# Sixteen matmuls that nobody reads, in TensorE's gaps at the end of a bandwidth-bound decode kernel

## The chip, the cores and the metric

The kernel runs on one core of a Trainium2 chip. The metric is the device time in microseconds (us) of one execution; a median over the runs of a set is quoted. Each run has a state: slow, for a program on one core, when it is over 1.5% above the fastest run of the same kernel, else fast; a single run has none. Ratios are the mean time of one kernel's fast runs over that of the other's of the same rounds, so not quite the ratio of the medians that stand beside them.

## The reference, cut to what matters

One decode step, cut to its outline: grouped-query attention over a long cache (part A), a small gated MLP (part B), and a gate that mixes the two.

```python
q = x @ wq                                    # 1 x 1024 -> 32 heads of 128
scores = einsum(q, k) * 128 ** -0.5           # 4 kv heads, 65536 cached tokens, 128 wide
a = softmax(scores) @ v ... @ wo              # wo: 4096 x 1024
b = mlp(x)                                    # w_in, w_out
return g * a + (1 - g) * b
```

What matters is the traffic: one token of query meets all of k_cache, v_cache, wq, w_in, w_out and wo, each read once. The profile counts 162.01 MB from HBM.

## The kernel before

All large operands go through one SBUF tile `kv` of five slots, loaded by one queue (SyncE) in program order. Each kv head has four K tiles and four V tiles. The end of the kernel is the part that the change touches:

```python
WO_SPLIT = ((16,), (8, 4, 2, 1, 1))
...
    for j, n, at in ((0, 2, 1), (2, 1, 3), (3, 1, 4)):       # the last head's V tiles
        for i, vt in enumerate(load_kv(A_v_cache, G - 1, j, at, n)):
            v_tile(G - 1, j + i, vt)
    head_out(G - 1)                                          # DVE chain and two small matmuls
    ...
    for at, split in enumerate(WO_SPLIT):
        for n in split:                                      # wo in pieces of 16, 8, 4, 2, 1, 1 rows
            t = load(wo_view[:, c0:c0 + n, :], (n, D), ...)
            project(t, n, oa, c0, last=(c0 + n == OC))       # 4 matmuls a row, 32 columns x 256
            c0 += n
    ...
    nc.scalar.copy(out=out_sb[:], in_=out_ps[:])             # eviction, then two small writes
```

The split of wo into ever smaller pieces means that only one row, four matmuls, stands after the last landing.

Of the kernel before, what the change touches and what calls it, by code (L numbers as in the profile page):

```python
# [8 lines left out]
FP32 = mybir.dt.float32  # L9
# [6 lines left out]
P = 128  # L16
# [6 lines left out]
ZN = 448  # L23
HN = 512
WO_SPLIT = ((16,), (8, 4, 2, 1, 1))


@with_exitstack
def kernel(
# [15 lines left out]
    nc = tc.nc  # L45

    _, _, D = A_x.shape
    _, G, S, DH = A_k_cache.shape
# [15 lines left out]
    assert S % (P * CT) == 0 and F == 2 * NB * ZN and ZN == B * FC and HD == NHB * NB * HN  # L64
    assert NHB * NB == 2 * G and CC * B == 2 * HN and sum(map(sum, WO_SPLIT)) == OC

# [5 lines left out]
    pss = ctx.enter_context(tc.tile_pool(name="pss", bufs=2, space=bass.MemoryType.PSUM))  # L72
# [6 lines left out]
    def same_weights(ins):  # L79
        held.add(ins.ins.name)  # L80
# [79 lines left out]
    def load(src, shape, at):  # L160
        n = 1
        for s in shape:
            n *= s
        v = kv[:, int(at * CT * P):int(at * CT * P) + n]
        if len(shape) == 2:
            v = v.rearrange("p (a b) -> p a b", b=shape[1])
        ins = nc.sync.dma_start(out=v, in_=src)  # L167
        if not first_load:
            first_load.append(ins.ins.name)
        return v  # L170

    def load_kv(src, g, j, at, n=1):
        h, i = divmod(j, 2)
        rows = src[0, g, 2 * h * CT * P:2 * (h + 1) * CT * P, :].rearrange(
            "(p c) d -> p (c d)", c=2 * CT)
        v = load(rows[:, i * CT * DH:(i + n) * CT * DH], (n * CT * DH,), at)
        return [v[:, i * CT * DH:(i + 1) * CT * DH] for i in range(n)]
# [26 lines left out]
    wt = [big.tile([P, VC, BP, NB, VC, REP], BF16, name=f"wt{i}") for i in range(2)]  # L204
# [15 lines left out]
    def one_hot(shape, dtype, in0, col, name):  # L220
# [13 lines left out]
                     start=True, stop=True)  # L234
# [107 lines left out]
    for k in range(NHB):  # L342
# [15 lines left out]
                     rhs=q4[:].rearrange("p t x -> p (t x)"), start=True, stop=True)  # L358
# [71 lines left out]
    def v_tile(g, j, vt):  # L430
        if j == 0:
            o_ps[g] = pso.tile([P, 2, VC * DH], FP32, name="o_ps")
        vx = vt.rearrange("p (v c d) -> p c v d", v=VC, d=DH)
        for u in range(CC // 2):
            hs = slice(u % 2 * P // 2, (u % 2 + 1) * P // 2)
            for e in range(2):
                ins = nc.tensor.matmul(  # L437
                    o_ps[g][hs, e, :],
                    lhsT=ptt[g, j][:, 2 * u:2 * u + 2, :].rearrange("p c x -> p (c x)"),
                    rhs=vx[:, 2 * u + e], start=(j == 0 and u < 2),  # L440
                    stop=(j == NT - 1 and u >= CC // 2 - 2), skip_group_check=True)
                if e > 0:
                    same_weights(ins)

    def head_out(g):
        gs = slice(g * B, (g + 1) * B)
        nc.vector.tensor_tensor(  # L447
            out=om8, in0=o_ps[g][:].rearrange("p e (v d) -> p (e v) d", d=DH),
            in1=own_8[:].unsqueeze(2).to_broadcast([P, 2 * VC, DH]), op=ALU.mult)
        o_sb = wk.tile([P, DH], FP32, name="o_sb")  # L450
        nc.vector.tensor_reduce(out=o_sb[:], in_=om8.rearrange("p x d -> p d x"), axis=AX.X,  # L451
                                op=ALU.add)
        om_ps = psm.tile([P, DH + NT], FP32, name="om_ps", tag="m")
        hs = hsel[:].rearrange("p h q -> p (h q)")
        nc.tensor.matmul(om_ps[gs, DH:], lhsT=hs, rhs=lss[g][:], start=True, stop=True,
                         skip_group_check=True)
        nc.tensor.matmul(om_ps[gs, :DH], lhsT=hs, rhs=o_sb[:], start=True, stop=True,  # L457
                         skip_group_check=True)
        rl = wk.tile([P, 2], FP32, name="rl")
        nc.vector.reduce_sum(out=rl[gs, 0:1], in_=om_ps[gs, DH:], axis=AX.X)  # L460
        nc.vector.reciprocal(out=rl[gs, 1:2], in_=rl[gs, 0:1])
        om = wk.tile([P, QD, OC], FP32, name="om")
        nc.vector.tensor_tensor(
            out=om[gs], in0=om_ps[gs, :DH].rearrange("p (q c) -> p q c", c=OC),
            in1=own_q[gs, :].unsqueeze(2).to_broadcast([B, QD, OC]), op=ALU.mult)
        osum = wk.tile([P, OC], FP32, name="osum")
        nc.vector.tensor_reduce(out=osum[gs, :], in_=om[gs].rearrange("p q c -> p c q"),
                                axis=AX.X, op=ALU.add)
        nc.vector.tensor_scalar(out=oa[gs, :], in0=osum[gs, :], scalar1=rl[gs, 1:2],
                                scalar2=gate[gs, :], op0=ALU.mult, op1=ALU.mult)  # L470

    NO = D // NB
    out_ps = psl.tile([P, NO], FP32, name="out_ps")

    def project(w, n, vec, c0, first=False, last=False):
        for c in range(n):
            for t in range(NB):
                nc.tensor.matmul(  # L478
                    out_ps[t * B:(t + 1) * B, :],
                    lhsT=vec[:, c0 + c:c0 + c + 1].to_broadcast([P, B]),  # L480
                    rhs=w[:, c, t * NO:(t + 1) * NO],
                    start=(first and c == 0), stop=(last and c == n - 1),
                    skip_group_check=True)
# [22 lines left out]
    for j, n, at in ((0, 2, 1), (2, 1, 3), (3, 1, 4)):  # L506
        for i, vt in enumerate(load_kv(A_v_cache, G - 1, j, at, n)):
            v_tile(G - 1, j + i, vt)
    head_out(G - 1)


    wo_view = A_wo.rearrange("(p c) n -> p c n", c=OC)
    c0 = 0
    for at, split in enumerate(WO_SPLIT):
        for n in split:
            t = load(wo_view[:, c0:c0 + n, :], (n, D), at + c0 % (OC // 2) * D / (CT * P))
            project(t, n, oa, c0, last=(c0 + n == OC))
            c0 += n
    out_sb = const.tile([P, NO], BF16, name="out_sb")
    out_rows = out.rearrange("o t (q n) -> (o t q) n", n=NO)  # L520
    nc.scalar.copy(out=out_sb[:], in_=out_ps[:])  # L521
    for i, queue in enumerate((nc.scalar, nc.sync)):
        p0 = (2 * i + 1) * B - 1
        ins = queue.dma_start(out=out_rows[2 * i:2 * i + 2, :], in_=out_sb[p0:p0 + 2, :])
# [40 lines left out]
```

## Time and profile before

| | before |
|---|---|
| median of the first three runs | 383.22 us (383.17 to 383.25) |
| HBM read | 162.01 MB at 425 GB/s over the span of 381.4 us |
| TensorE busy | 232.4 us, 61% |
| DVE busy | 218.4 us, 57% |
| last wo transfer lands | 378.88 us after the span's start |

Three more lines of the page; the first is what moved, the others the chain of work that ended last, as shares of the span by engine, and the eviction (its idle time before it, and what ended that):

```profile
HBM read 162.01 MB, written 0.00 MB: 425 GB/s over the span
...
DMA 59%; PE 20%; DVE 16%; issue 2%; ACT 1%; SPq 1%; DVEq 0%; ACTq 0%
...
L521 ACT CAST out_sb<-out_ps 128x256 bf16<-128x256 f32 x1 | 0.4, 372 | 45.4 <-PE out_ps L478 45.4
```

The chain lists PE at 20% and DVE at 16% because buffers in mid-kernel come free through them.

### The profile page before, as it was taken

To read this page: it belongs to the slowest core of one execution; us is meant where nothing else is said; L and a number is where in the kernel's file an instruction comes from. 1 tells how busy PE (TensorE), PEld (TensorE's weight loads), DVE (VectorE), ACT (ScalarE), POOL (GpSimd) and SP (SyncE) were. 2 spreads that over 40 slices of the span, in tenths; PEclk is the share of its full clock that TensorE was granted. 3 is DMA by queue.
4 is the path that set the end of the run, shared out by engine and by line. 5 is a ranking of instruction groups with operands and counts; after the bars stand their busy time and mean duration, and the time that the engine had idled before them with its cause. 6 is when DMAs were issued, how large, how long until landed. Compare 5 with 4: busy or idle time off the path is not lost.

```text
span 381.4 us, 2581 instructions
## 1 busy us (share of the span) xinstructions
PE 232.4 (61%) x1372; PEld 56.8 (15%) x796; DVE 218.4 (57%) x211; ACT 39.6 (10%) x55; POOL 4.4 (1%) x10
## 2 busy tenths in 40 slices
PE   0433467678157944796397629872967196849355
PEld 0110011112011210121011101120111011212123
DVE  4241487996687506966977059669780488550040
ACT  1010001111601100114010001050001010500000
POOL 4000000000000000000000000000000000000000
PEclk9966659998759895989588959895799679969766
DMA  9999999999999999999999999999999999999995
GB/s 376 439 426 416 433 436 440 436 461 429 400 426 440 440 435 426 440 440 440 440 428 440 440 440 433 428 427 406 433 440 428 426 433 427 440 411 436 440 405 230
DMA packets 4375, 162.17 MB, mean 425 GB/s; under 512 B 520, under 2 KB 524, under 8 KB 908
## 3 DMA queue, kind: packets, MB, share of 16 engines
q1 hardware_dynamic: 4324, 162.01, 98.7%
q8 instruction: 8, 0.13, 0.1%
q14 instruction: 3, 0.02, 0.0%
q10 hardware_dynamic: 40, 0.01, 0.0%
HBM read 162.01 MB, written 0.00 MB: 425 GB/s over the span
## 4 chain that ended last, share of the span: by engine, by line
DMA 59%; PE 20%; DVE 16%; issue 2%; ACT 1%; SPq 1%; DVEq 0%; ACTq 0%
DMA kv<-in_A_k_cache_dram 37%; PE s_ps L391 15%; DVE kv L384 9%; DMA kv<-in_A_wo_dram 8%; DMA kv<-in_A_wq_dram 7%; DMA kv<-in_A_v_cache_dram 7%; PE o_ps L437 3%; DVE pt L427 2%; DVE mx L386 1%; DVE o_sb L451 1%; PE q_ps L277 1%; ACT sc L424 1%; DVE rowt L447 1%; ACT sc L402 1%; SPq L167 1%
## 5 line engine op out<-in xcount | busy, mean ns | idle before, releaser
L391 PE MATMUL s_ps<-kv,wt 128*128 128x512 bf16 x512 | 142.1, 437 | 81.8 <-DVE kv L384 81.7
L384 DVE STREAM_TRANSPOSE kv<-kv 128x2048 int32<-128x2048 int32 x64 | 142.7, 2280 | 55.5 <-DMA kv<-in_A_k_cache_dram 55.5
L437 PE MATMUL o_ps<-kv,pt 128*64 128x512 bf16 x512 | 61.6, 399 | 7.7 <-DMA kv<-in_A_v_cache_dram 7.7
L391 PEld LDWEIGHTS <-wt 128*128 128x128 bf16 x256 | 27.5, 108 | 197.6 <-issue 140.2
L402 ACT CAST sc<-s_ps 128x1024 bf16<-128x1024 f32 x16 | 16.2, 1013 | 253.5 <-PE s_ps L391 253.5
L437 PEld LDWEIGHTS <-pt 128*64 128x64 bf16 x256 | 16.0, 115 | 50.7 <-issue 48.1
L427 DVE STREAM_TRANSPOSE pt<-sc 128x1024 bf16<-128x1024 bf16 x16 | 18.6, 1217 | 6.8 <-ACT sc L424 6.8
L386 DVE TENSOR_REDUCE mx<-sc 128x1 f32<-128x1024 bf16 x12 | 14.5, 1207 | 10.1 <-ACT sc L402 10.1
L424 ACT ACTIVATE sc<-sc,nb 128x1024 bf16<-128x1024 bf16 x16 | 18.2, 1137 | 12.2 <-DVE nb L420 12.2
L447 DVE TENSOR_TENSOR rowt<-o_ps,own 128x1024 f32<-128x1024 f32 x4 | 4.8, 1194 | 24.9 <-PE o_ps L437 24.9
L457 PE MATMUL om_ps<-o_sb,hsel 128*32 128x128 f32 x8 | 2.5, 421 | 19.7 <-DVE o_sb L451 19.7
L406 DVE TENSOR_REDUCE mx<-sc 128x1 f32<-128x1024 bf16 x4 | 4.9, 1220 | 14.2 <-ACT sc L402 14.2
L277 PE MATMUL q_ps<-kv,xT 128*32 128x512 bf16 x64 | 7.2, 627 | 7.4 <-DMA kv<-in_A_wq_dram 7.4
L478 PE MATMUL out_ps<-kv,oa 128*32 128x256 bf16 x128 | 6.7, 366 | 3.7 <-DMA kv<-in_A_wo_dram 2.2
L277 PE MATMUL z_ps<-kv,xT 128*32 128x448 bf16 x64 | 6.2, 570 | 3.8 <-DMA kv<-in_B_w_in_dram 3.8
L344 DVE TENSOR_TENSOR rowt<-q_ps,own_b 128x512 f32<-128x512 f32 x2 | 1.3, 686 | 12.5 <-PE q_ps L277 12.5
L451 DVE TENSOR_REDUCE o_sb<-rowt 128x128 f32<-128x1024 f32 x4 | 7.5, 1872 | 0.1
L292 DVE TENSOR_TENSOR rowt<-z_ps,own_b 128x448 f32<-128x448 f32 x2 | 1.2, 620 | 8.5 <-PE z_ps L277 8.5
L233 PE MATMUL xb_ps<-xg,spread 8*128 8x256 bf16 x1 | 0.4, 367 | 9.1 <-DMA xg<-in_gate_w_dram 9.1
L277 PEld LDWEIGHTS <-xT 128*32 128x32 bf16 x64 | 3.0, 139 | 19.4 <-issue 19.3
L478 PEld LDWEIGHTS <-oa 128*32 128x32 bf16 x128 | 4.4, 124 | 6.1 <-issue 3.3
L521 ACT CAST out_sb<-out_ps 128x256 bf16<-128x256 f32 x1 | 0.4, 372 | 45.4 <-PE out_ps L478 45.4
(88 smaller groups left out, 54.8 us busy)
## 6 DMA issues: line engine op xcount, KB each, us to landing
kv<-in_A_k_cache_dram SPq DMA_DIRECT2D x4, 4096.0 KB, 26.8
kv<-in_A_wq_dram SPq DMA_DIRECT2D x2, 4096.0 KB, 32.8
kv<-in_A_v_cache_dram SPq DMA_DIRECT2D x2, 4096.0 KB
kv<-in_B_w_in_dram SPq DMA_DIRECT2D x2, 3584.0 KB, 15.0
kv<-in_A_wo_dram SPq DMA_DIRECT2D x1, 4096.0 KB
kv<-in_B_w_out_dram SPq DMA_DIRECT2D x1, 3584.0 KB
kv<-in_A_wo_dram SPq DMA_DIRECT2D x1, 2048.0 KB, 28.6
kv<-in_A_wo_dram SPq DMA_DIRECT2D x1, 1024.0 KB, 30.7
```

Of the source, the lines that this page charges most:

```text
L277: ins = nc.tensor.matmul(ps[t * B:(t + 1) * B, k * HN:k * HN + n], lhsT=xT[:, i * KH + c:i * KH + c + 1].to_broadcast([P, B]), rhs=w[:, c, ...
L384: nc.vector.transpose(out=kb[:, v * n:(v + 1) * n], in_=kb[:, v * n:(v + 1) * n])
L386: nc.vector.reduce_max(**late.pop())
L391: ins = nc.tensor.matmul(s_ps[:, k * HN:(k + 1) * HN], lhsT=wt[g % 2][:, v, b].rearrange("p a v h -> p (a v h)"), rhs=kx[:, b // 2, b % 2, ...
L402: nc.scalar.copy(out=sct[g, j][:], in_=s_ps[:])
L406: nc.vector.reduce_max(**late.pop())
L424: nc.scalar.activation(out=sct[g, j][:], in_=sct[g, j][:], func=ACT.Exp, scale=SCALE, bias=nb[:, 0:1], accum_out=lss[g][:, j:j + 1])
L427: nc.vector.transpose(out=ptt[g, j][:].rearrange("p c x -> p (c x)"), in_=sct[g, j][:])
L437: ins = nc.tensor.matmul(o_ps[g][hs, e, :], lhsT=ptt[g, j][:, 2 * u:2 * u + 2, :].rearrange("p c x -> p (c x)"), rhs=vx[:, 2 * u + e], sta ...
L447: nc.vector.tensor_tensor(out=om8, in0=o_ps[g][:].rearrange("p e (v d) -> p (e v) d", d=DH), in1=own_8[:].unsqueeze(2).to_broadcast([P, 2 ...
L451: nc.vector.tensor_reduce(out=o_sb[:], in_=om8.rearrange("p x d -> p d x"), axis=AX.X, op=ALU.add)
L478: nc.tensor.matmul(out_ps[t * B:(t + 1) * B, :], lhsT=vec[:, c0 + c:c0 + c + 1].to_broadcast([P, B]), rhs=w[:, c, t * NO:(t + 1) * NO], st ...
```

## The change

The granted clock is the share of full speed that the profile shows for TensorE. In the profile before it falls to 0.50 at 377.48 us, after 3.41 us in which TensorE was busy for only 45%, and stays there to the end. The intent: matmuls of no use, "fillers", put into the gaps of the tail, should hold the clock up, so that the real matmuls of the tail run at full speed.

```diff
+WO_BUSY = {16: 4, 8: 2, 4: 1, 2: 1, 1: 0}
...
+    def keep_busy(n):
+        ps = pss.tile([P, 2 * HN], FP32, name="busy_ps", tag="s")
+        w = wt[G % 2][:].rearrange("p v b t u h -> p (v b t u h)")
+        for i in range(n):
+            ins = nc.tensor.matmul(ps[:, :HN], lhsT=w[:, :P], rhs=w[:, :HN], start=True,
+                                   stop=True, skip_group_check=True)
+            if i > 0:
+                same_weights(ins)
...
+    keep_busy(4)
     head_out(G - 1)
+    keep_busy(4)
...
             project(t, n, oa, c0, last=(c0 + n == OC))
+            keep_busy(WO_BUSY[n])
             c0 += n
```

## The prediction

> **What bounds the kernel now.** I read the page first, then the chain of work that ended last, then the timeline of the tail, then the windows that follow the grid of the TensorE clock. From the page, the slices and the chain:
>
> ```profile
> PE   0433467678157944796397629872967196849355
> PEclk9966659998759895989588959895799679969766
> DMA  9999999999999999999999999999999999999995
> GB/s 376 439 426 416 433 436 440 436 461 429 400 426 440 440 435 426 440 440 440 440 428 440 440 440 433 428 427 406 433 440 428 426 433 427 440 411 436 440 405 230
> ```
>
> TensorE is half idle and its granted clock moves between slices, but the DMA row is 9 in every slice but the last, and the rate hardly leaves 400 to 440 GB/s whatever the clock does. 162.01 MB come from HBM at 425 GB/s, and those bytes are the time. The chain in order of time says the same of the end:
>
> ```profile
> 345.20 0.33 SPq L167
> ...
> 347.00 31.88 DMA kv<-in_A_wo_dram
> 378.88 0.04 issue
> 378.92 0.43 PE out_ps L478 x3
> 379.35 0.02 issue
> 379.37 0.37 ACT out_sb L521
> ```
>
> The last wo transfer is issued at 347.00 and lands at 378.88, and only then come the last four matmuls (0.43 us; the chain counts three of them), the eviction (0.37 us) and the output's write, which begins at 379.77 and ends with the span at 381.4. Nothing that TensorE does between 347.00 and 378.88 can move the landing, since all six wo loads are already queued. Their buffers came free through the second V tile, at 345.19; the first added matmul comes after the fourth V tile, at 365. The part of the tail that TensorE can still touch is thus what follows the landing: 0.43 us.
>
> The timeline of the tail, columns start, duration, engine, line, output and input, count, and in brackets the idle time before with what ended it:
>
> ```profile
> 359.20 5.92 PE L437 MATMUL o_ps<-kv,pt 128*64 128x512 bf16 x32 [6.08 <-DMA kv<-in_A_v_cache_dram]
> ...
> 368.34 0.64 PE L457 MATMUL om_ps<-o_sb,hsel 128*32 128x128 f32 x2 [3.07 <-DVE o_sb L451]
> ...
> 370.37 4.62 PE L478 MATMUL out_ps<-kv,oa 128*32 128x256 bf16 x96 [1.39 <-DVE oa L469]
> ...
> 376.33 0.62 PE L478 MATMUL out_ps<-kv,oa 128*32 128x256 bf16 x16 [1.34 <-DMA kv<-in_A_wo_dram]
> ...
> 377.60 1.08 PE L478 MATMUL out_ps<-kv,oa 128*32 128x256 bf16 x12 [0.64 <-DMA kv<-in_A_wo_dram]
> ...
> 378.92 0.41 PE L478 MATMUL out_ps<-kv,oa 128*32 128x256 bf16 x4 [0.24 <-DMA kv<-in_A_wo_dram]
> ```
>
> The three last brackets are what matters. TensorE is done before each of the last transfers and waits 1.34, 0.64 and 0.24 us for DMA. These gaps are what the change fills, and they are also its slack.
>
> **What the Trainium skill says.** "TensorE: Matmul & The Clock Gate", Part 1: the clock is at half rate until a free-running window of 3413 ns was busy, and falls back after an idle one. The trace agrees: the clock of this tail changes at about 363.83, 367.24, 374.07 and 377.48, all on one grid of 3.41 us. The windows on that grid (busy time of PE, PEld, DVE, ACT, POOL, then clock, DMA share, GB/s):
>
> ```profile
> 360.42:363.83 3.41, 3.41 (x18) 0.93 (x8) 0.00 (x0) 0.00 (x0) 0.00 (x0) 0.50 0.98 423
> 363.83:367.24 3.41, 1.45 (x14) 0.41 (x6) 2.05 (x2) 0.00 (x0) 0.00 (x0) 1.00 1.04 447
> 367.24:370.66 3.42, 0.92 (x10) 0.42 (x14) 2.25 (x6) 0.00 (x0) 0.00 (x0) 0.50 0.90 383
> 370.66:374.07 3.41, 3.41 (x72) 2.54 (x68) 0.00 (x0) 0.00 (x0) 0.00 (x0) 0.50 0.97 406
> 374.07:377.48 3.41, 1.54 (x48) 1.15 (x41) 0.00 (x0) 0.00 (x0) 0.00 (x0) 1.00 0.88 342
> 377.48:380.90 3.42, 1.42 (x16) 0.50 (x15) 0.00 (x0) 0.37 (x1) 0.00 (x0) 0.50 0.11 41
> ```
>
> A full window (3.41 busy) is followed by clock 1.00. A window with 1.45 or 1.54 us busy, 43% and 45%, is followed by 0.50. I laid the same grid over the whole span: from 15 us on, no window above 47% was followed by a fall, and those at 41% and less were; between 43% and 47% it went both ways. So it is no rule of full idleness: about half of a window busy keeps a running clock up. For the rise, 75% was once not enough and 83% was.
>
> The same page, "Back-to-back issue gap": N/1.2 ns cold and N/2.4 + 2.5 warm, so 427 and 216 ns for a 512-column matmul. The trace has no such unpaired full-width matmuls in the tail, but the V tile agrees: 22 of its matmuls, two at a time in 64 columns each, take 4.62 us at clock 0.50, which is 420 ns a pair.
>
> "DMA: Bandwidth & Descriptors", "Where 436 GB/s comes from", gives 435 GB/s as the ceiling of the SBUF ports. The page's row stands at 426 to 440 in most slices, so there is nothing to win from the transfers.
>
> **The change part by part.** It removes nothing. By the order of instructions, DVE, ScalarE, SyncE and GpSimd are the same; TensorE gets sixteen 128x512 matmuls in six groups of 4, 4, 4, 2, 1, 1, with one weight load each. They go to the two PSUM buffers of the scores, which are long free. A wait of a group names TensorE's own semaphore, for the group two before, which is over by then. The operands are mostly zero (they are the last even head's weight tile, of which a small part is set); the result is never read.
>
> The cost of each group, on the transfers' old times, with 0.216 us a matmul warm and 0.427 cold, and 30.5 ns for each small projection matmul warm (56 of them took 1.71 us at clock 1.00 at 94.21) against 54 ns cold (64 in the 3.46 us from 370.37 to 373.83):
>
> First 4, after the V tile ends at 365.1 with the clock up: 4 x 0.216 = 0.86 us, to 366.0. DVE runs meanwhile (its 1.23 and 1.87 us started on the V tile, not on the added work); TensorE is wanted next at 368.34. Cost 0. Window 363.83 to 367.24 goes from 1.45 to 2.31 us, 68%: the clock stays up.
>
> Second 4, from about 368.9 to 369.8; the head's output is ready at 370.3. Cost 0. That window has then about 0.55 + 0.86 + 0.3 = 1.7 us, 50%: it just stays up.
>
> Projection of 16 rows: 64 x 30.5 ns = 1.95 us instead of 3.46, from 370.37 to 372.3. Third 4 to 373.2, then the wait for the 8 rows, which by their issue at 345.20 and 28.6 us to landing come at 373.8. The 32 matmuls: 0.98 us, to 374.8. Then 2: 0.43 us, to 375.2. The next rows come at 376.3 as before. 16 matmuls, 0.5 us, to 376.8, one filler to 377.0; rows at 377.6; 8 matmuls and one filler to about 378.1; the row before last needs TensorE from 378.28. Every filler ends before the next transfer. Window 374.07 to 377.48 gets 0.73 + 0.43 + 0.5 + 0.22 = 1.9 us, 55%, instead of 45%: so the last window should stay warm.
>
> The gain: on the path stand only the last four matmuls. One took a median of 407 ns in this tail and 273 ns at clock 1.00 around 94 us, and the four run nearly side by side, so 0.43 us becomes about 0.30: a gain of 0.13 us. The 1.5 us saved on the 16 rows and the rest turn into longer waits for DMA. The sum is 383.22 - 0.13 = 383.09 if the clock is up at the end, and 383.22 if it isn't. I give the clock three chances in four and take 383.1.
>
> **The rivals.** One: the fillers are late and delay the last rows. If everything ran cold, the second 4 would end at 370.7, the 16 rows at 374.2, the third 4 at 375.9, the 8 rows at 377.6, two fillers at 378.5, the 4 rows at 379.3, a filler at 379.8, and the last rows, with one more filler, near 381: some 1.7 us late, 384.9. Against it: such a TensorE would be busy without a gap, and the trace shows the clock rise after every full window, so it can't stay cold beyond one. A mixed case, with a late rise and one filler in front of the last rows, costs at most one cold filler, 0.43 us: 383.6. Two: the clock falls anyway, because zeros in fillers count for less than the real work or because half a window is not enough. Then the tail is as it was, 383.2; the windows at 43 to 47% that went both ways speak for this. Three: TensorE's extra reads from SBUF slow the transfers. Each per cent of the rate in the last 15 us would be 0.15 us. Against it: the rate was 426 GB/s with TensorE nearly idle (355 to 360) and 439 while it was busy (345 to 350). Four: the whole tail speeds up by the microseconds that the projection saves, say 1.5 us, 381.7. Against it stand the three DMA waits in the timeline; none of that time is on the path.
>
> **Range and chances.** The three runs of before span 0.08 us. The gain lies between 0 and 0.15, a late filler could cost up to 0.4, and another set of runs could lie 0.2 off. So 382.8 to 383.5. A 2% verdict needs 7.7 us, more than the whole tail after the last V tile could give outside of its transfers, and no rival comes near it on either side: same 0.985, faster 0.005, slower 0.01.
>
> **What would show it.** In the changed profile the DMA and GB/s rows should be as before and the last wo transfer should land within some tenths of 378.9; the clock from 368 to 380 should be 1.0 with perhaps one window of 0.5; the first 96 projection matmuls should take about 3 us without their fillers in place of 4.62, with longer DMA waits in front of the later ones; the last four should take about 0.30 us. If the wait in front of the last four is gone, rival one holds. If they still take 0.41, rival two does. If the last landing is later, it is rival three. A time outside the range would mean that TensorE's clock touches the transfers, which I see no sign of.

## The result, and the profile after

The changed kernel takes 383.16 us (383.04 to 383.36, 6 runs); the kernel before 383.24 (383.09 to 383.29, 6 runs). The ratio is 0.9999 with a 95% interval of 0.9986 to 1.0012: the same.

Clock, DMA and rate of the changed kernel, from the slices of its page:

```profile
PEclk9999859999759885999598959896889688969689
DMA  9999999999999999999999999999999999999995
GB/s 382 440 423 423 423 436 440 437 475 422 400 419 440 440 442 440 433 426 440 433 435 440 440 440 433 421 427 406 440 433 442 440 412 434 433 407 440 437 409 229
```

The DMA row is the same, digit for digit. The clock of the last three slices is 6, 8 and 9 tenths, where before it was 7, 6 and 6. The chain in order of time, at its end:

```profile
346.40 32.54 DMA kv<-in_A_wo_dram
378.94 0.04 issue
378.98 0.32 PE out_ps L488 x4
379.30 0.02 issue
379.32 0.37 ACT out_sb L534
```

The last landing is at 378.94 (378.88 before). What TensorE owes after it is 0.32 us in place of 0.43. From the landing to the eviction's start it is 379.32 - 378.94 = 0.38 us, against 379.37 - 378.88 = 0.49: the gain is 0.11 us. The timeline of TensorE's tail (start, duration, line, count, in brackets the wait before):

```profile
364.45 1.04 PE L477 MATMUL busy_ps<-wt 128*128 128x512 bf16 x4
365.42 0.23 PE L456 MATMUL om_ps<-ls,hsel 128*32 128x4 f32 x2
367.74 0.41 PE L458 MATMUL om_ps<-o_sb,hsel 128*32 128x128 f32 x2 [2.10 <-DVE o_sb L452]
368.08 1.04 PE L477 MATMUL busy_ps<-wt 128*128 128x512 bf16 x4
369.54 3.50 PE L488 MATMUL out_ps<-kv,oa 128*32 128x256 bf16 x64 [0.43 <-DVE oa L470]
...
376.40 0.62 PE L488 MATMUL out_ps<-kv,oa 128*32 128x256 bf16 x16 [0.87 <-DMA kv<-in_A_wo_dram]
...
377.66 0.40 PE L488 MATMUL out_ps<-kv,oa 128*32 128x256 bf16 x8 [0.31 <-DMA kv<-in_A_wo_dram]
...
378.98 0.29 PE L488 MATMUL out_ps<-kv,oa 128*32 128x256 bf16 x4 [0.36 <-DMA kv<-in_A_wo_dram]
```

The waits for DMA in front of the 4, the 2 and the last row are still there, shorter by the fillers (0.87, 0.31) or longer by the faster matmuls (0.36 in place of 0.24). The last four take 0.29 us in place of 0.41. One line is not as hoped: the 64 matmuls of the 16 rows took 3.50 us, as slowly as before. The clock's grid says why. In each of the twelve profiles all changes of the clock lie on one grid of 3.413 us, to within 0.001 us by the traces' clock records; where the grid starts differs from run to run. The windows on it in this run (PE busy first, then PEld, DVE, ACT, POOL, and the clock third from the end):

```profile
365.94:369.36 3.42, 1.38 (x6) 0.23 (x3) 2.82 (x6) 0.00 (x0) 0.00 (x0) 1.00 0.89 378
369.36:372.77 3.41, 3.23 (x64) 2.42 (x64) 0.13 (x1) 0.00 (x0) 0.00 (x0) 0.51 0.97 411
372.77:376.18 3.41, 2.77 (x46) 1.05 (x35) 0.00 (x0) 0.00 (x0) 0.00 (x0) 0.99 0.99 393
376.18:379.60 3.42, 2.20 (x34) 0.96 (x33) 0.00 (x0) 0.28 (x1) 0.00 (x0) 1.00 0.36 137
```

In this run the grid lies so that one window holds the whole wait for DVE's chain: 1.38 of 3.42 us busy, 40%, and the next window is cold, that is, at clock 0.5. The fillers from 372.98 on then bring 81% and the clock is up until the end.

### The profile page after: what moved, and what is told of

Read it like the earlier page. It is cut to its first block, busy times and chain, and to the rows that moved or that the text cites. A ratio compares the mean times of both kernels' runs of the same rounds, so it can differ in the third digit from the quotient of the medians.

```text
span 381.4 us, 2603 instructions
## 1 busy us (share of the span) xinstructions
PE 231.5 (61%) x1388; PEld 56.5 (15%) x802; DVE 218.3 (57%) x211; ACT 39.6 (10%) x55; POOL 4.4 (1%) x10
## 4 chain that ended last, share of the span: by engine, by line
DMA 60%; DVE 18%; PE 17%; issue 2%; ACT 1%; SPq 1%; DVEq 0%; ACTq 0%
DMA kv<-in_A_k_cache_dram 37%; PE s_ps L392 12%; DVE kv L385 12%; DMA kv<-in_A_wo_dram 9%; DMA kv<-in_A_wq_dram 7%; DMA kv<-in_A_v_cache_dram 7%; PE o_ps L438 3%; DVE pt L428 2%; DVE mx L387 2%; DVE o_sb L452 1%; PE q_ps L278 1%; ACT sc L425 1%; DVE rowt L448 1%; ACT sc L403 1%; SPq L168 1%
## 5 line engine op out<-in xcount | busy, mean ns | idle before, releaser
L392 PE MATMUL s_ps<-kv,wt 128*128 128x512 bf16 x512 | 139.5, 430 | 85.3 <-DVE kv L385 85.2
L438 PE MATMUL o_ps<-kv,pt 128*64 128x512 bf16 x512 | 60.3, 393 | 7.9 <-DMA kv<-in_A_v_cache_dram 7.9
## 6 DMA issues: line engine op xcount, KB each, us to landing
kv<-in_A_wo_dram SPq DMA_DIRECT2D x1, 2048.0 KB, 29.2
```

What stands on the lines that cost most here:

```text
L392: ins = nc.tensor.matmul(s_ps[:, k * HN:(k + 1) * HN], lhsT=wt[g % 2][:, v, b].rearrange("p a v h -> p (a v h)"), rhs=kx[:, b // 2, b % 2, ...
L438: ins = nc.tensor.matmul(o_ps[g][hs, e, :], lhsT=ptt[g, j][:, 2 * u:2 * u + 2, :].rearrange("p c x -> p (c x)"), rhs=vx[:, 2 * u + e], sta ...
```

## The experiments

Theory: the last landing sets the end; TensorE's clock counts only for the four matmuls after it, and the fillers cost nothing because each ends before the next landing. Rivals: that TensorE's tail is not on the path at all; that the clock must be held from the head on; that the early tail is on the path; that zeros count for less than data; and that the small pieces of wo are what costs the tail. Each of e1 to e8 had 5 runs; in each of two sets, the kernel before had 9 runs with a median of 383.18 us. Every ratio's interval lies within 2% of 1; what tells the theories apart is inside the tail.

### e1: four fillers on the path

```diff
-            keep_busy(WO_BUSY[n])
+            keep_busy(4 if c0 == OC - 2 else WO_BUSY[n])
```

> The changed kernel with four more fillers between the row before last and the last row of wo. My theory (the end is the last landing plus what TensorE still owes then; the old fillers all fit into waits): the gap there was 0.36 us, four fillers at full clock issue in 0.86 us, so the last four matmuls start about 0.4 to 0.5 us after the landing and the time is 383.16 + 0.45 = about 383.6; the wait for DMA in front of them is gone. If the clock were down there, +1.3 us. Rival (TensorE at the end is not on the path, the output's write or a transfer hides it): unchanged, 383.2.

Measured: 383.74 us (383.61 to 383.84), 0.50 to 0.58 above the changed kernel's two medians; ratio to before 1.0012 (1.0000 to 1.0025). The chain's end:

```profile
378.47 0.97 PE busy_ps L477 x4
379.44 0.25 PE out_ps L488 x4
379.69 0.02 issue
379.71 0.37 ACT out_sb L534
```

No DMA stands right before the last four any more; they wait for the fillers. The last landing is at 378.79 in this run (the trace's landing record), so from it to the eviction it is 0.92 us, against 0.38 in the changed kernel: 0.54 more, as the medians have it. So TensorE is on the path after the last landing, and the rival that the output's write hides it falls.

### e2: fillers in the last gaps only

```diff
-WO_BUSY = {16: 4, 8: 2, 4: 1, 2: 1, 1: 0}
+WO_BUSY = {16: 0, 8: 2, 4: 1, 2: 1, 1: 0}
...
     def keep_busy(n):
+        if n == 0:
+            return
...
-    keep_busy(4)
     head_out(G - 1)
-    keep_busy(4)
```

> Only the fillers after the pieces of 8, 4 and 2 rows (2, 1, 1); none around the head and none after the 16 rows. My theory: the clock of the last window is decided by the window before it alone, which goes from 45% to some 60% busy, so the last four matmuls take about 0.29 us as in the changed kernel, and the time is that of the changed kernel, 383.1 to 383.2. Rival (the clock has to be held up from the head on): last four 0.41 us as before.

Measured: 383.18 us (383.11 to 383.21), ratio 0.9998 (0.9984 to 1.0011). The last windows of the grid in this run:

```profile
370.91:374.32 3.41, 3.41 (x72) 2.62 (x64) 0.00 (x0) 0.00 (x0) 0.00 (x0) 0.50 0.99 408
374.32:377.74 3.42, 2.40 (x55) 1.30 (x46) 0.00 (x0) 0.00 (x0) 0.00 (x0) 1.00 0.84 325
377.74:381.15 3.41, 1.18 (x17) 0.36 (x16) 0.00 (x0) 0.37 (x1) 0.00 (x0) 1.00 0.07 25
```

The projection of the 16 rows ran at half clock, as before; the window after it was 2.40 of 3.42 us busy, 70%, and the last window kept clock 1.00. The last four took 0.29 us. In this profile four fillers thus do what sixteen do, and the clock need not be held from the head on.

### e3: the head's gap filled as well

```diff
-    keep_busy(4)
+    keep_busy(10)
     head_out(G - 1)
-    keep_busy(4)
+    keep_busy(5)
```

> 10 and 5 fillers around the head in place of 4 and 4. My theory: the window that was 40% busy in the changed kernel gets over half, so the clock no longer falls there and the projection of 16 rows takes about 2.0 us instead of 3.50, ending 1.5 us earlier; none of it reaches the end, as the rows after it wait for DMA: time 383.1 to 383.2. Rival (the early part of the tail is on the path): about 1.5 us faster, 381.7.

Measured: 383.20 us (383.05 to 383.28), ratio 0.9998 (0.9986 to 1.0011). The window around the head, columns as above:

```profile
365.98:369.39 3.41, 2.59 (x14) 0.37 (x5) 2.81 (x6) 0.00 (x0) 0.00 (x0) 1.00 0.87 370
```

TensorE's next work, from the timeline:

```profile
369.62 1.93 PE L488 MATMUL out_ps<-kv,oa 128*32 128x256 bf16 x64 [0.21 <-DVE oa L470]
...
373.94 1.06 PE L488 MATMUL out_ps<-kv,oa 128*32 128x256 bf16 x32 [1.42 <-DMA kv<-in_A_wo_dram]
```

The grid lies as in the changed kernel's profile (365.98 against 365.94). With 76% busy in place of 40% the clock stayed up, and the 16 rows took 1.93 us in place of 3.50. All that was saved is found again in front of the next 32 matmuls, which begin at 373.94 in both runs, now after a wait of 1.42 us for DMA. The early tail is not on the path. The earlier work also empties a later window: by the trace, TensorE was busy for 1.59 us, 47%, of the window from 372.90 to 376.31, where it was 80% in the changed kernel. That was still enough for a clock of 1.00 at the end.

### e4: random data in place of zeros

```diff
-        w = wt[G % 2][:].rearrange("p v b t u h -> p (v b t u h)")
+        w = kv[:, 4 * CT * P:5 * CT * P]
```

> The same fillers with weights and moving data taken from the last V tile (random numbers) in place of the mostly zero weight tile. My theory: busy is busy; durations of fillers, the clock of the tail and the time as in the changed kernel, last four about 0.29 us, 383.1 to 383.2. Rival (zeros count for less in the activity that holds the clock): with data the clock does not fall at all from 366 us on, and the 16 rows take 2.0 us; still the same time, as the transfers bound it.

Measured: 383.10 us (383.08 to 383.16), ratio 0.9996 (0.9984 to 1.0009). Its grid, too, lies as in the changed kernel; the window around the head, and then the timeline's line of the 16 rows:

```profile
365.94:369.36 3.42, 1.38 (x6) 0.23 (x3) 2.82 (x6) 0.00 (x0) 0.00 (x0) 1.00 0.87 369
```

```profile
369.51 3.50 PE L488 MATMUL out_ps<-kv,oa 128*32 128x256 bf16 x64 [0.42 <-DVE oa L470]
```

The same 1.38 us busy, the same fall of the clock and the same 3.50 us follow with random numbers, and the clock of the end is 1.00 in both. At this phase of the grid mostly-zero fillers and random ones have the same effect on this one core; the rival falls.

### e5, e6, e7: larger last pieces of wo

Here the last pieces of wo were made larger, e5 and e7 with the fillers (none after the last piece), e6 without. The question was whether the fillers, with a faster TensorE after the landing, make room for a better split.

```diff
-WO_SPLIT = ((16,), (8, 4, 2, 1, 1))
+WO_SPLIT = ((16,), (8, 4, 4))      # e5 with fillers, e6 without
+WO_SPLIT = ((16,), (8, 4, 2, 2))   # e7 with fillers
```

> The changed kernel with the second half of wo in pieces of 8, 4, 4 rows instead of 8, 4, 2, 1, 1 (fillers 4, 4, 4, 2, 1 stay, none after the last). Larger pieces mean packets of 8 KB instead of 2 and 4 KB at the very end, where the rate falls to some 200 GB/s. Theory A (small packets cost the tail of the transfers): the last landing comes some 0.5 us earlier; against it 16 matmuls instead of 4 stand after it, 0.62 us at full clock instead of 0.30: about 0.2 us faster to 0.1 slower. Theory B (the fall of the rate is only the drain of the queues): landing unchanged, 0.3 us slower, 383.5.

> The kernel before with 8, 4, 4 rows and no fillers. Here the clock after the landing matters more: 16 matmuls cold take about 0.95 us against 0.62 at full clock. If the window before the end is under half busy the clock is down and this is some 0.3 us slower than the same split with fillers; if not, equal to it.

> The changed kernel with 8, 4, 2, 2 rows. Theory A (small packets cost): landing 0.2 us earlier, 8 matmuls after it take 0.40 instead of 0.30 us: 0.1 us faster, 383.05. Theory B (drain): landing unchanged, 0.1 us slower.

Measured: e5 383.64 us (383.34 to 383.80, ratio 1.0011, 0.9998 to 1.0023), e6 383.70 us (383.65 to 383.80, ratio 1.0014, 1.0002 to 1.0027), e7 383.23 us (383.19 to 383.24, ratio 1.0002, 0.9988 to 1.0015). The chain's end in e5 and then in e6:

```profile
378.72 0.04 issue
378.76 0.64 PE out_ps L488 x16
...
379.43 0.37 ACT out_sb L534
```

```profile
378.70 0.04 issue
378.74 1.07 PE out_ps L478 x14
...
379.83 0.37 ACT out_sb L521
```

The last landing comes at 378.72 and 378.70, and in e7 at 378.81. Against the landings with the finest split, 378.73 to 378.98 over the eight profiles of the table below, that is early, but not by the 0.5 us of theory A; in e5 and e6 what stands after the landing grows more. So the finest split beats 8, 4, 4, and by these landings its small packets cost under 0.3 us. Against 8, 4, 2, 2 nothing is decided: e7's 383.23 and e8's 383.24 are the same time. The pair also shows the clock's worth where more work follows the landing: the same 16 matmuls (the chain of e6 counts 14 of them) take 0.64 us with the clock up and 1.07 with it down, 0.43 us. In the profiles e5's eviction starts 0.40 us before e6's, yet the medians differ by only 0.06 us. The profiled run of e5, at 383.34, is the fastest of its five, with one more at 383.39, while the other three stand at 383.64 to 383.80, like e6's, so its clock may not have been up in all of them; only one run of each kernel has a profile, so this stays open.

### e8: the changed kernel again; e9 and e10: the kernel before again

> The changed kernel unchanged, for the spread between sets of runs and a second look at the clock, whose grid starts at another phase. Ratio to before 0.9995 to 1.0000; the last four matmuls at 0.29 us; the clock may fall in another window around the head.

> The kernel before once more, one look at the clock of its tail at another phase of the clock's grid. My theory: without fillers some window around the end is under half busy at most phases, so the last four matmuls take about 0.41 us and the chain from the last landing to the eviction 0.49 us. If the phase happens to keep the clock up, they take 0.29 us and 0.38 us, and the gain of the change is then none.

> The same, a second look: 0.41 us at clock 0.5 or 0.29 us at clock 1.0 for the last four matmuls, by the phase; the landing at 378.7 to 379.0 in either case.

Measured: e8 383.24 us (383.06 to 383.53), ratio 1.0002 (0.9990 to 1.0015); e9 one run, 383.25 us; e10 one run, 383.12 us. The chain's end in e8 and in e10:

```profile
378.79 0.04 issue
378.83 0.32 PE out_ps L488 x4
379.15 0.02 issue
379.18 0.37 ACT out_sb L534
```

```profile
378.73 0.04 issue
378.77 0.43 PE out_ps L478 x4
379.20 0.02 issue
379.23 0.37 ACT out_sb L521
```

All looks together:

| profile | last landing | eviction starts | between | last window starts | busy in the window before it | clock at the end |
|---|---|---|---|---|---|---|
| before | 378.88 | 379.37 | 0.49 | 377.49 | 45% | 0.50 |
| e9, before again | 378.84 | 379.33 | 0.49 | 377.52 | 44% | 0.50 |
| e10, before again | 378.73 | 379.23 | 0.50 | 376.34 | 40% | 0.50 |
| changed | 378.94 | 379.32 | 0.38 | 376.23 | 80% | 1.00 |
| e8, changed again | 378.79 | 379.18 | 0.39 | 375.83 | 84% | 1.00 |
| e2, four fillers | 378.94 | 379.32 | 0.38 | 377.74 | 70% | 1.00 |
| e3, filled head | 378.98 | 379.36 | 0.38 | 376.31 | 47% | 1.00 |
| e4, random data | 378.90 | 379.28 | 0.38 | 376.20 | 80% | 1.00 |

(The last window is that of the grid in which the last four matmuls run. The grids are taken from the traces' clock records; the windows shown further up were set by eye and lie up to 0.1 us beside them.)

The column "between" parts the kernels cleanly: 0.49 to 0.50 us without fillers, 0.38 to 0.39 with them. The last landing wanders by 0.25 us from run to run, over twice the gain. In e10 the grid lay a third of a window (some 1.1 us) away from that of the first profile of before, and the clock was down at the end all the same.

A rival is left that no run was made for: that the phase of the grid, and not the fillers, sets the clock of the end. The traces answer it, as some grids happen to coincide. The last two windows of e10, without fillers, and of e3, with them:

```profile
372.92:376.34 3.42, 1.37 (x44) 1.01 (x43) 0.00 (x0) 0.00 (x0) 0.00 (x0) 1.00 0.99 392
376.34:379.75 3.41, 2.20 (x32) 0.93 (x24) 0.00 (x0) 0.37 (x1) 0.00 (x0) 0.50 0.33 123
...
372.90:376.31 3.41, 1.59 (x34) 0.96 (x33) 0.00 (x0) 0.00 (x0) 0.00 (x0) 1.00 0.98 392
376.31:379.72 3.41, 2.21 (x34) 0.96 (x33) 0.00 (x0) 0.36 (x1) 0.00 (x0) 1.00 0.34 130
```

(The changed kernel's own last window starts 0.11 us before e10's, with 80% in the window before it.) In the same way e1's last window starts at 377.47, where that of before starts at 377.49: 65% busy in the window before it and clock 1.00, against 45% and 0.50. So at each of these two phases the fillers make the difference. Other phases of the kernel before were not seen (e9, meant for one, fell on that of the first profile), so whether it keeps its clock up at some of them stays open.

## Why the prediction was right

**What bounds the kernel.** Right. The DMA row did not change, the last landing moved within its own spread, and e3 shows 1.57 us of TensorE time saved before the landing with nothing of it in the total.

**The path.** Right: only what follows the landing counts. e1 put four fillers, 0.97 us, across it and the time rose by 0.50 to 0.58 us. (One reading of the chain is wrong, without effect: the last wo buffers came free through the first V tile of the last head, and not the second. Of its 64 matmuls from 339.76 on, the chain counts 32 up to 345.19.)

**The gain.** The forecast was 0.13 us; the profiles show 0.11 (0.43 to 0.32 in the chain). The medians show 0.08 less in the first set and 0.06 more in the second, so the time itself does not resolve the gain; only the profile does. The forecast time, 383.1, was met by 383.16 and missed a little by 383.24, both inside the range.

**The clock.** Right for the end, wrong in the middle. The step that failed is the working of the second 4 ("it just stays up") and with it the 1.95 us for the 16 rows: in the changed kernel's profile a window of 40% let the clock fall and the rows took 3.50 us. The working took the old profile's grid for granted, while the grid falls elsewhere in each run. That the phase is the cause can be checked, as in e1, with the same fillers around the head, the grid lay within 0.03 us of the old one:

```profile
363.81:367.23 3.42, 2.37 (x18) 0.49 (x7) 2.10 (x2) 0.00 (x0) 0.00 (x0) 1.00 1.04 446
367.23:370.64 3.41, 1.94 (x28) 0.78 (x28) 2.19 (x6) 0.00 (x0) 0.00 (x0) 1.00 0.94 399
```

That is 69% and 57%, where the prediction has 68% and 50%; the clock stayed up and the rows took 1.93 us, as they did in e5. So the working holds at the phase that it assumed. In the four other profiles with these fillers around the head (changed, e4, e7, e8) the last window starts at 375.83 to 376.23 in place of 377.26 to 377.47, and the rows took 3.44 to 3.51 us. The error did not reach the total, as none of that work is on the path; the prediction's last paragraph had allowed for one window at 0.5. At the end the clock held with more to spare than the 55% of the working in the changed kernel (80%), and with less in e3 (47%).

**The fillers' length.** A group of four was put at 0.86 us; from its first start to the next instruction the profile shows 365.42 - 364.45 = 0.97 us. That every filler ends before the next transfer was not quite so: the third group ran until 373.94, while the 8 rows had landed by about 373.8 (issued at 344.60, with 29.2 us to landing), and no wait for DMA stands before their matmuls. The next wait, 0.87 us, made up for it.

**The rivals.** Late fillers (one): the wait in front of the last four grew from 0.24 to 0.36 us, so no. A clock that falls anyway (two): in the middle yes, at the end in none of the eight profiles with fillers in the last gaps. Slower transfers (three): 425 GB/s in both. (Single slices of both rows reach 440 and more, above the 435 that the prediction names as the ceiling, so they do not show where the ceiling lies; that there was nothing to win rests on the full DMA row.) That the landings with fillers lie on average some 0.1 us later than those without (378.91 over five, 378.82 over three) is within the spread, and e5 against e6, 378.72 against 378.70, does not repeat it; a difference under 0.1 us is left open. A faster tail as a whole (four): e3 rules it out.

No version tried beats both kernels by more than the spread between sets. e2 has the changed kernel's tail with 4 fillers in place of 16.

## What to carry to other kernels

Before warming TensorE's clock, find the last transfer and count what TensorE owes after it: that alone can be won, here 0.43 us of 383, of which the clock was worth 0.11. Where warming pays, fill the gaps of the last window or two: in e2 the clock was 0.50 up to 374.32 and 1.00 at the end all the same. Give each filler less time than the wait that it fills, and look at more than one profile, as the grid of the clock starts elsewhere in each run. A gain below the spread of the landing has to be read in the profile as a difference between two events of the same run, as the medians can't show it.

## What the Trainium skill lacked or had wrong

- "TensorE: Matmul & The Clock Gate", Part 1, says that the clock falls after an idle window. In these runs it fell after windows that were far from idle: 40% busy in the changed kernel (1.38 of 3.42 us), 43% and 45% in the kernel before. Windows of 70% and 76% (e2, e3) kept it up, and so did one of 47% (e3, from 372.90). With the windows of all twelve profiles laid on their grids, the highest share before a fall is 44.9% (before, from 374.08) and the lowest that kept the clock up 39.8% (e8, from 160.80); for the rise, 77.9% was once not enough (e8, from 338.30) and 77.7% once was (e5, from 18.90). The page gives no share at which the clock falls or rises.
- The same page says that benchmarks need random data, since zeros do not trip a limiter on a die with three busy cores. It does not say whether zeros count as activity for the clock. On one core they do, as far as the mostly-zero operands here show it: a group of four took 1.04 us and the clock of the tail fell and rose in the same windows with them and with random data (e4).
- The same page, "Back-to-back issue gap", gives N/2.4 + 2.5, so by estimate 0.86 us for four 512-column matmuls. From the first of a group to the next instruction of another kind the runs show 0.97 us, at clock 1.00, and for e3's group of ten 366.78 - 364.51 = 2.27 us. Six more thus cost 1.30 us, 0.217 each, as the formula has it; what is left, some 0.1 us a group, goes with the change from one kind of matmul to the next, for which the page has no figure.
